# A planned RWKV and MLP kernel: four of its 24 units get their r and k turned by VectorE instead of TensorE, and the plan is searched in another way

## The chip, the cores and the metric

The kernel runs on one core of one Trainium2 chip. What counts is the device time of one execution in microseconds: the median over several runs. All engines of a core (TensorE or PE, VectorE or DVE, ScalarE or ACT, GpSimd or POOL, and SyncE or SP, which here only starts transfers) run at once, each through its own queue in order, and wait for one another by semaphores.

## What is computed

Two stages follow each other: a recurrent attention (RWKV5) over 768 steps, for 4 sequences with 8 heads of 48 numbers, and then a layer with 2048 hidden values on its 3072 rows of 384 numbers.

```python
def _attn_ref(r, k, v, w, u):
    B, H, S, D = r.shape                      # 4, 8, 768, 48
    state = np.zeros((B, H, D, D), dtype=np.float32)
    for t in range(S):
        kt, vt, rt = (k[:, :, t], v[:, :, t], r[:, :, t])
        cur = np.einsum('bhd,bhe->bhde', u[None] * kt, vt)
        y[:, :, t] = np.einsum('bhd,bhde->bhe', rt, state + cur)
        state = w[None, :, :, None] * state + np.einsum('bhd,bhe->bhde', kt, vt)
    return y

def _moe_ref(x, w_in, w_out):                 # 384 -> 2048 -> 384
    h = x @ w_in
    g = h - np.tanh(h)
    return (g @ w_out).astype(np.float32)
```

r, k and v are float32 on input; the two weight matrices come as float64 and are converted on the chip.

## The kernel before

**Units.** The attention is cut into 24 units. A unit is 64 steps of two sequences (z is 0 or 1), all heads: unit n has chunk n // 2 and the pair of sequences n % 2. Two units make a block of 256 rows for the layer, so there are 12 blocks j = 0 to 11, and block j needs units 2j and 2j + 1. Units of the same pair follow one another through their state.

A unit loads r, k and v with the steps on the partitions (`fetch`). It scales k by the powers of the decay (`kw`, DVE), and needs r and k once more with the head's 48 numbers on the partitions, r scaled by the powers of w, k by their inverse: `rT` and `kT`. Then TensorE makes r times state (`from_state`) and the products of r and k within the chunk (`levels`), DVE copies those below the diagonal into `at` under a mask (L981), the diagonal comes from `own`, `own_sum` and ScalarE's `diagonal`, and TensorE makes the outputs from `at` and v and the new part of the state from kw and v (`outputs`, `to_state`). ScalarE copies the result to `xt` and `rest`, and six small transfers on GpSimd's queue (`fill`, L931) put `rest` into xt; with that a block can be used.

**Two ways to turn.** In the first way, TensorE transposes r and kw into PSUM (`turn`, L795, two groups of four transposes per unit), DVE scales r from there (`scale_r`, L799, by the table `w_up`), and ScalarE copies k (`copy_k`, L832). In the other way, `spread_out` (L813) loads r and k a second time from DRAM in blocks of 32 steps by 32 numbers, eight transfers for r and eight for k on SP's queue, and DVE turns each 32 x 32 block and scales the whole (`across`, L818 and L819). The blocks lie in memory that the partial sums `parts` of the first six layer blocks used before. Here too r and k are loaded with the steps on the partitions, for kw and the diagonal. Between from_state and levels ScalarE reads one number of the PSUM bank (`between`, L872). Before the change, units 0 to 15 go the first way and 16 to 23 the other.

**The layer.** A tile is a block and two slices of 128 hidden values: TensorE makes h in PSUM (L169), ScalarE s, th, tg, q and small (squares, tanh and a mask), DVE g, c1, c2 and cp (L193 to L199), and TensorE multiplies g with w_out. There are 96 tiles. The first six blocks go through three passes, of 4, 4 and 8 slices; the partial sums of the first two lie in `parts`. In the first two passes the product with w_out is plain (o, L207). From the third pass on it is Strassen's scheme with seven products instead of eight (`products`, p, L258), for which GpSimd forms sums of g (`sums_of_g`, L243 to L247) and which collects its outputs on DVE (L286, L290 `gather`, the step that adds `parts` for the last time). It takes four PSUM banks, among them those of the first way's transposes, so the third pass begins only after the last unit of the first way has left them (`done`). The weights' conversion (L137 to L143) and the combinations of w_out (`mix`, L267) are work of DVE and ScalarE in the first 250 us.

**The order.** No loop sets the order. `near` adds every step to a `Plan` as a task with an engine, an assumed cost, its predecessors and a due time. `Plan.forward` lists the tasks by simulated time and due time, `backward` makes due times from a plan, and `search` moves due times at random and keeps what does not lengthen the planned span. `Plan.order` first searches 2500 times for the work that fits before 240 us (`BUSY`), then 500 times for the whole, then exchanges the tasks of units 16 to 23 for those of the other way (`change`), makes the due times after 240 us anew and searches 500 times there. Instructions are issued in the resulting order on each engine.

Of the kernel before, what the change touches and what calls it, by code (L numbers as in the profile page):

```python
# [31 lines left out]
C = 128  # L32
# [9 lines left out]
SEVEN = 8  # L42

# [258 lines left out]
class Plan:  # L302
# [12 lines left out]
    def __init__(self):  # L315
        self.tasks, self.fills, self.changes = [], [], []

    def add(self, engine, cost, run, after=(), due=1e9, data=0, gated=False, steps=0):
        t = SimpleNamespace(engine=engine, cost=cost, run=run, after=[x for x in after if x], due=due, data=data,
                            gated=gated, steps=steps, then=[], n=len(self.tasks))  # L320
        for x in t.after:
            x.then.append(t)
        self.tasks.append(t)
        return t

    def change(self, t, **new):

        self.changes.append((t, new))
# [149 lines left out]

    def order(self, first=2500, tries=500):
# [18 lines left out]
        self.search(due, tries, chance, 0.0)  # L498

        for t, new in self.changes:  # L500
            for x in t.after:
                x.then.remove(t)
            vars(t).update(new)
            t.after = [x for x in t.after if x]
            for x in t.after:
                x.then.append(t)
        for _ in range(4):
            plan = self.forward(self.due)
            latest = self.backward(plan)
            self.due = [old if start < self.BUSY else new for old, new, start in zip(self.due, latest, plan[1])]  # L510
        plan = self.search(self.due, tries, chance, self.BUSY)
# [28 lines left out]
def near(ctx, tc, r, k, v, w, u, out, shared, moe_w_in, moe_w_out):  # L540
# [20 lines left out]
    plan = Plan()  # L561
    add = plan.add
# [6 lines left out]

    spread = parts.rearrange("q a n -> q (a n)")  # L570
    blocks = [spread[:, i * 512 : (i + 1) * 512].rearrange("q (x b e) -> q x b e", x=2 * NP, b=SHORT // 32) for i in range(4)]
    again = spread[:, 2048 : 2048 + NP * (SHORT + 1)].rearrange("d (p n) -> d p n", p=NP)
# [83 lines left out]
    inverse = work.tile([128, NP, SHORT + 1], F32, name="inverse", tag="tg")  # L656
    w_up = fixed("w_up", [128, NP, 2, SHORT])
# [25 lines left out]
    def fills(to):  # L683
        def run(n):
# [6 lines left out]
    now = [add(e, 1.25 if e == "ACT" else .87, lambda e=e, at=at, x=x: e_of[e].dma_start(out=rows[at : at + NP, :, :D], in_=x.rearrange("(p i) d -> p i d", i=2)), due=-1, data=.05)  # L691
           for e, at, x in (("SP", 0, w), ("ACT", NP, u))]
    cols = add("PE", .25, lambda: T.transpose(cols_ps, rows.rearrange("p i d -> p (i d)"), ident[: 2 * NP, : 2 * NP]), now)


    now = add("DVE", .45, lambda: V.tensor_scalar(
        by[:, :, 1:], wcol[:, :, None].to_broadcast([128, NP, SHORT]), W_LOW, W_HIGH, ALU.max, ALU.min), [cols])
    now = add("DVE", .7, lambda: V.tensor_tensor_scan(
        power.rearrange(flat), by.rearrange(flat), plus.rearrange(flat), 0.0, ALU.mult, ALU.add), [now])

    ups = add("ACT", .6, lambda: A.copy(w_up, power[:, :, None, :SHORT].to_broadcast([128, NP, 2, SHORT])), [now])
    now = add("DVE", 1.75, lambda: V.reciprocal(inverse, power), [now])
    inverted = now
    doubled = add("ACT", .6, lambda: A.copy(twice, inverse[:, :, None, 1:].to_broadcast([128, NP, 2, SHORT])), [now])
    now = tabled = add("PE", .7, table, [doubled], steps=8)
    downs = add("ACT", .5, lambda: A.copy(w_down, tab.rearrange("s (h d) -> s h d", h=H)[:, :, :D]), [now])
    keeps = add("ACT", .2, lambda: A.copy(saved, cols_ps), [cols])
    w_us = add("POOL", .2, lambda: G.tensor_tensor(w_u, saved[:, :NP], saved[:, NP:], ALU.mult), [keeps])
    now = add("POOL", 1.0, bounds, [keeps])
    now = add("PE", .2, lambda: T.matmul(tab[0:1, 0:1], ok[:, 0, :1], shared["one"], start=True, stop=True), [now, downs])  # L710
    flagged = add("DVE", .15, lambda: V.tensor_scalar(shared["flag"], tab[0:1, 0:1], 128 * NP - 0.5, None, ALU.is_lt), [now])
    bonus = add("SP", .65, lambda: Q.dma_start(
        out=ub.rearrange("p h d -> p (h d)"),
        in_=bass.AP(tensor=u.tensor, offset=u.offset, ap=[[0, 128], [1, H * D]])), data=.7)

    add("ACT", 1.3, lambda: A.activation(fixed("warm", [128, 1]), shared["one"], AF.Tanh), due=0)


    def steps(generator):

        made = []

        def step():
            if not made:
                made.append(generator())
            next(made[0])

        return step

    loads, converted = [], []  # L730
    for n in range(weights.count):

        queues, data = (("SP",), (3.0,)) if n % 4 > 1 else (("SP", "POOL") * 2, (1.2, .95) * 2)
        of = [add(e, .55, lambda n=n, i=i, e=e: weights.load(n, i, e_of[e]), [converted[n - 4] if n >= 4 else None],
                  data=x, gated=True) for i, (e, x) in enumerate(zip(queues, data))]
        if weights.sources[n % 4 > 1].dtype != I64:
            converted.append(of[-1])
            continue
        step = steps(lambda n=n: weights.convert(n))
        now = of + ([converted[n - 2]] if n >= 2 else [])  # L740
        for name, cost in (("DVE", .47), ("DVE", .47), ("ACT", .84), ("ACT", .84), ("DVE", .87), ("DVE", .87), ("DVE", .87)):
            now = [add(name, cost, step, now)]
        converted += now


    def flat4(t):
        return t.rearrange("d p z t -> d (p z t)")

    def put(*args, **how):
        T.matmul(*args, skip_group_check=True, **how)  # L750

    units, filled, last_h = [], {}, {}

    def unit(n):
# [3 lines left out]
        ch, half = divmod(n, 2)  # L758
        j, slot = divmod(n, L)
        steps_at = slice(ch * SHORT, (ch + 1) * SHORT)  # L760
        t = SimpleNamespace(at=ats[n % 2])
        rt, vt, kw, state = rts[n % (AHEAD + 1)], vts[n % (AHEAD + 1)], kws[n % 2], states[half]
        two = n >= L * (FIRST + 2)
        pair = yk_ps if two else x_banks[n == 1]
        sign = -1.0 if slot and j in dense.negative else 1.0
        r_ps, k_ps = (pair[:, i] for i in range(2))
        lev, own_lev = (pair[:, :, at : at + 256].rearrange("s i (p t) -> s i p t", p=NP) for at in ((256, 0) if two else (0, 256)))
        none = SimpleNamespace(**{x: None for x in "r k v turn rT kw kT rk du own diag state lev cp out xt rest add decay".split()})
        b1, b2, b3 = (units[n - i] if n >= i else none for i in (1, 2, 3))
        x = SimpleNamespace(rest=None, rk=None, du=None, own=None)  # L770
        units.append(x)
        product = n < OWN
        swap = n >= SWAP


        direct = j == 0

        def fetch(name, src, after):
            def run(z):
                if name == "k" and not hasattr(t, "kt"):  # L780
                    t.kt = first_k[slot] if direct else load.tile([128, H, D], F32, name="kt", tag="kt")
                to = {"r": rt, "v": vt}.get(name)
                Q.dma_start(out=(t.kt if to is None else to)[HALF[z], :, :D],  # L783
                            in_=src[half * 2 + z, :, steps_at, :].rearrange("h t d -> t h d"))

            of = [add("SP", .65, lambda z=z: run(z), after, data=.71) for z in range(2)]
            return add("none", 0, lambda: None, of)

        x.r = fetch("r", r, [b3.turn, b3.rk, b1.r])
        x.k = fetch("k", k, [b3.kw, b3.rk, b1.k])  # L790
        x.v = fetch("v", v, [b3.out, b1.v])

        def turn(src, to):
            for p in range(NP):
                T.transpose(to[:, p * C : (p + 1) * C], src[:, 2 * p : 2 * p + 2, :].rearrange("t h d -> t (h d)"), ident)  # L795

        def scale_r():
            t.rT = work.tile([128, NP, 2, SHORT], F32, name="rT", tag="rT")
            V.tensor_tensor(flat4(t.rT), r_ps, flat4(w_up), ALU.mult)  # L799

        def scale_k():
            t.kT = work.tile([128, NP, 2, SHORT], F32, name="kT", tag="kT")
            V.tensor_tensor(t.kT, k_ps.rearrange("d (p z t) -> d p z t", p=NP, z=2),
                            inverse[:, :, None, 1:].to_broadcast([128, NP, 2, SHORT]), ALU.mult)
# [17 lines left out]
        def across_r():  # L822
            t.rT = across("rT", 0, power[:, :, :SHORT])
# [46 lines left out]
        def between():  # L870

            A.copy(seen, y_ps[:1, :, 0, 0])  # L872
# [552 lines left out]
```

## Time and profile before

| | us |
|---|---|
| median of three runs | 591.49 (590.93 to 591.64) |
| profiled execution | 591.61 |
| its span, first to last instruction | 589.5 |
| TensorE busy | 571.2 |
| weight loads busy (they overlap with matmuls) | 485.0 |
| VectorE busy | 484.1 |
| ScalarE busy | 398.9 |
| GpSimd busy | 208.3 |

The profile is of one execution. An engine's busy time is the union of its instructions' durations; ends of matmuls are modelled, so on TensorE the distance between starts says more than a duration. In lists of groups, a line has the source line, engine and operation, the tile written and those read, the shape, the count, the busy time, the mean in ns, and the engine's idle time just before. In the timeline a line has start, length, engine, line, operation, tiles and count, and in brackets how long the engine was idle before and which instruction released it. TensorE's small matmuls of a unit have the line of a helper, L750. The chain of waits is followed back from the last instruction.

### The profile page before, as it was taken

What the parts mean: (1) busy time and instruction counts of PE and PEld (TensorE: products, weight loads), DVE (VectorE), ACT (ScalarE), POOL (GpSimd) and SP (SyncE); (2) the same over time, 40 slices, a digit from 0 to 9 for tenths busy, and PEclk for the clock granted to TensorE, in tenths of its full rate; (3) what the DMA queues carried; (4) which work ended last, traced back from release to release, by engine and by line L of the source; (5) the groups of instructions that cost most, each with busy time, mean ns of one, the idle gap of its engine ahead of it and who ended that gap; (6) DMA issues with size and microseconds to landing.
All of it is one profiled execution on the core that took longest, in us unless ns stands there. A gap on an engine that the chain in (4) does not pass through costs nothing.

```text
span 589.5 us, 14312 instructions
## 1 busy us (share of the span) xinstructions
PE 571.2 (97%) x5525; PEld 485.0 (82%) x5525; DVE 484.1 (82%) x806; ACT 398.9 (68%) x894; POOL 208.3 (35%) x366
## 2 busy tenths in 40 slices
PE   8888999999999989999999999999999999999996
PEld 5566677777777768999999998989999888999995
DVE  5699969999999999988779889697775896555666
ACT  3698888989686975775555566565665785476652
POOL 6002212201000143555554544483344554363420
PEclk9999999999999999999999999999999999999999
DMA  6976995954411310203111412244121220100101
GB/s 118 201 155 129 161 204 107 126 132 86 93 54 28 62 30 21 39 16 61 36 26 24 85 28 30 40 83 69 35 30 19 38 40 1 25 11 2 28 1 31
DMA packets 121141, 36.91 MB, mean 63 GB/s; under 512 B 113352, under 2 KB 115496, under 8 KB 121064
## 3 DMA queue, kind: packets, MB, share of 16 engines
q1 hardware_dynamic: 115900, 28.73, 26.9%
q0 software_dynamic: 4992, 6.99, 5.4%
q8 instruction: 45, 0.74, 0.5%
q14 instruction: 32, 0.26, 0.1%
q10 hardware_dynamic: 172, 0.20, 0.1%
HBM read 30.08 MB, written 4.72 MB: 59 GB/s over the span
## 4 chain that ended last, share of the span: by engine, by line
PE 76%; DVE 11%; ACT 4%; issue 3%; DMA 3%; SPq 2%; POOL 0%; DVEq 0%; ACTq 0%; POOLq 0%
PE h L169 37%; PE p L258 27%; PE o L207 5%; PE yk_ps L750 5%; SPq L783 2%; DMA st<-in_moe_w_in_dram 2%; DVE tg L197 1%; DVE g L193 1%; DVE tg L195 1%; DVE g L199 1%; DVE rT L799 1%; ACT at L844 1%; ACT s L178 1%; PE x_ps L795 1%; DMA kt<-in_k_dram 1%
## 5 line engine op out<-in xcount | busy, mean ns | idle before, releaser
L169 PE MATMUL h<-xt,w_in_sb 128*128 128x256 f32 x1152 | 281.0, 381 | 1.1 <-DVE w_in_sb L143 0.9
L169 PEld LDWEIGHTS h<-xt,w_in_sb 128*128 128x128 f32 x1152 | 212.9, 190 | 31.4 <-PE x_ps L795 1.1
L243 POOL TENSOR_TENSOR sg<-g 128x256 f32<-128x256 f32 x69 | 53.8, 780 | 144.6 <-DVE g L199 72.5
L258 PE MATMUL p<-mixed,sg 128*128 128x192 f32 x426 | 104.0, 326 | 0.0
L193 DVE TENSOR_TENSOR g<-h,th 128x512 f32<-128x512 f32 x96 | 65.8, 685 | 33.2 <-ACT s L178 14.3
L182 ACT ACTIVATE tg<-h 128x512 f32<-128x512 f32 x96 | 57.2, 596 | 48.3 <-PE h L169 48.2
L195 DVE SCALAR_TENSOR_TENSOR tg<-s,tg 128x512 f32<-128x512 f32 x96 | 68.3, 712 | 25.9 <-ACT tg L182 13.8
L180 ACT ACTIVATE th<-h 128x512 f32<-128x512 f32 x96 | 57.4, 598 | 43.0 <-PE h L169 42.8
L931 POOL DMA_DIRECT2D xt<-rest x66 | 32.3, 496 | 146.0 <-ACT rest L910 146.0
L178 ACT ACTIVATE s<-h 128x512 f32<-128x512 f32 x96 | 57.4, 598 | 39.1 <-PE h L169 38.8
L199 DVE COPY_PREDICATED g<-small,tg 128x512 f32<-128x512 int32 x96 | 76.0, 793 | 4.0
L258 PEld LDWEIGHTS p<-mixed,sg 128*128 128x128 f32 x426 | 75.1, 190 | 0.0
L197 DVE SCALAR_TENSOR_TENSOR tg<-q,tg 128x512 f32<-128x512 f32 x96 | 68.5, 715 | 7.5 <-ACT q L184 4.1
L207 PE MATMUL o<-w_out_sb,g 128*128 128x384 f32 x192 | 69.8, 490 | 1.7 <-DVE g L199 1.6
L258 PE MATMUL p<-w_out_sb,g 128*128 128x192 f32 x284 | 71.1, 332 | 0.0
L184 ACT ACTIVATE q<-s,m1b 128x512 f32<-128x512 f32 x96 | 69.5, 724 | 0.8
L186 ACT ACTIVATE small<-s,smallb 128x512 f32<-128x512 f32 x96 | 69.3, 722 | 0.5
L258 PEld LDWEIGHTS p<-w_out_sb,g 128*128 128x128 f32 x284 | 52.5, 190 | 7.4
L844 ACT ACTIVATE at<-same,du 128x64 f32<-128x64 f32 x184 | 47.7, 343 | 5.7 <-DVE du L840 5.6
L207 PEld LDWEIGHTS o<-w_out_sb,g 128*128 128x128 f32 x192 | 35.5, 190 | 18.4 <-issue 1.9
L245 POOL TENSOR_TENSOR sg<-sg,g 128x128 f32<-128x128 f32 x69 | 44.6, 647 | 5.1
L247 POOL TENSOR_TENSOR sg<-sg,g 128x128 f32<-128x128 f32 x69 | 39.0, 566 | 5.1
(131 smaller groups left out, 684.4 us busy)
## 6 DMA issues: line engine op xcount, KB each, us to landing
st<-in_moe_w_out_dram SPq DMA_DIRECT2D x8, 768.0 KB, 5.4
rt<-in_r_dram SPq DMA_DIRECT2D x48, 96.0 KB, 3.3
vt<-in_v_dram SPq DMA_DIRECT2D x48, 96.0 KB, 2.9
st<-in_moe_w_in_dram SPq DMA_DIRECT2D x16, 288.0 KB, 5.1
kt<-in_k_dram SPq DMA_DIRECT2D x44, 96.0 KB, 3.3
out_dram<-o POOLq DMA_DIRECT2D x44, 96.0 KB, 2.3
st<-in_moe_w_in_dram POOLq DMA_DIRECT2D x16, 96.0 KB, 5.1
xt<-rest POOLq DMA_DIRECT2D x66, 16.0 KB, 2.3
```

What stands on the lines that cost most here:

```text
L169: self.nc.tensor.matmul(t.h2[:, z], self.w_in_sb[:, t.f // 2, kk, z * 128 : (z + 1) * 128], self.xts[t.j][:, kk].rearrange("p b t -> p (b ...
L178: A.activation(out, t.h, AF.Square)
L180: A.activation(out, t.h, AF.Tanh)
L182: A.activation(out, t.h, AF.Tanh, scale=G1)
L184: A.activation(out, t.s, AF.Square, bias=self.m1b)
L186: A.activation(out, t.s, AF.Relu, bias=self.smallb, scale=-1.0)
L193: V.tensor_tensor(t.g, t.h, t.th, ALU.subtract)
L195: V.scalar_tensor_tensor(t.tg, t.s, C4, t.tg, ALU.mult, ALU.mult)
L197: V.scalar_tensor_tensor(t.tg, t.q, K1, t.tg, ALU.add, ALU.mult)
L199: V.copy_predicated(t.g, t.small.bitcast(I32), t.tg)
L207: self.nc.tensor.matmul(self.outs[i], t.g2[:, z, i * C : (i + 1) * C], self.w_out_sb[:, t.f + z, :], start=t.first and z == 0, stop=t.last ...
L258: self.nc.tensor.matmul(ps[bank][:, half * n : (half + 1) * n], a, b, start=t.first and half == 0, stop=t.last, skip_group_check=True)
```

## The change

`lay_out` now builds a plan for a given number of early units and a way to turn the later ones. It is called twice: once with 16 early units and TensorE turning all (`simpler`), which is searched as before but never run, and once with 12 early units, all others loaded in blocks of 32 and turned by DVE. The second plan takes from the first the due times of all tasks that start before 90 us (`ALIKE`), makes the others from the tasks' own due times, and searches 500 times over what lies after 90 us.

Units 12 to 15 thereby leave the first way. The four buffers for blocks lie over `parts` of layer blocks 0 to 2 only, since the inverse powers now have a place of their own, and the first two turned units wait for the gathers of those three blocks; before, the first two waited for the last products of blocks 0 to 3 in the third pass. The third pass waits for unit 11 and not 15. `w_up` goes: r is scaled by the powers with a broadcast. A path that gives some of a unit's elementwise work to GpSimd (`eased`) is there but with `EASED = 12` and 12 early units no unit takes it. Assumed costs in the plan change for turning (1.22 to 1.4) and mixing (0.47 to 0.65).

```diff
+ALIKE = 90.0
+EASED = 12
...
-    def change(self, t, **new):
-
-        self.changes.append((t, new))
...
+    def follow(self, other, until, tries=500):
+
+
+        theirs = {t.key: (other.due[t.n], t.start) for t in other.tasks}
+        kept = [theirs[t.key][0] if theirs.get(t.key, (0, until))[1] < until else None for t in self.tasks]
+
+        def pinned(due):
+            return [y if y is not None else x for x, y in zip(due, kept)]
+
+        due = [t.due for t in self.tasks]
+        for t in reversed(self.tasks):
+            for x in t.then:
+                due[t.n] = min(due[t.n], due[x.n] - t.cost - self.HOP - (self.LANDS if t.data else 0))
+        for _ in range(5):
+            plan = self.forward(pinned(due))
+            due = self.backward(plan)
+        return self.listed(self.search(pinned(due), tries, Random(5), until))
+
...
-    inverse = work.tile([128, NP, SHORT + 1], F32, name="inverse", tag="tg")
-    w_up = fixed("w_up", [128, NP, 2, SHORT])
+    inverse = fixed("inverse", [128, NP, SHORT + 1])
...
+    def lay_out(early, across_by):
+
+        plan = Plan()
...
-    ups = add("ACT", .6, lambda: A.copy(w_up, power[:, :, None, :SHORT].to_broadcast([128, NP, 2, SHORT])), [now])
+        ups = add("ACT", .6, lambda: None, [now])
...
-        two = n >= L * (FIRST + 2)
+            two = n >= early
+            turned = two and across_by == "DVE"
...
-            V.tensor_tensor(flat4(t.rT), r_ps, flat4(w_up), ALU.mult)
+                V.tensor_tensor(t.rT, r_ps.rearrange("d (p z t) -> d p z t", p=NP, z=2),
+                                power[:, :, None, :SHORT].to_broadcast([128, NP, 2, SHORT]), ALU.mult)
...
-            if n == L * (FIRST + 2):
-                V.reciprocal(again, power)
-            t.kT = across("kT", 1, again[:, :, 1:])
+                t.kT = across("kT", 1, inverse[:, :, 1:])
...
-        x.turn = add("PE", .46, lambda: turn(rt, r_ps), [x.r] + free, steps=8)
-        if two:
-            freed = [tiles[y].o for y in parted[:4]] if n < L * (FIRST + 3) else []
-            plan.change(x.turn, engine="SP", cost=4.8, run=lambda: spread_out(r, 0), after=[b2.rT, *freed], data=.8, steps=0)
...
+            if turned:
+                freed = sum((gathered[y] for y in range(3)), []) if n < early + 2 else []
+                in_r = add("SP", 4.8, lambda: spread_out(r, 0), [b2.rT, *freed], data=.8)
+                in_k = add("SP", 4.8, lambda: spread_out(k, 1), [b2.kT, *freed], data=.8)
+            x.turn = None if turned else add("PE", .46, lambda: turn(rt, r_ps), [x.r] + free, steps=8)
...
-        x.rT = add("DVE", .62, scale_r, both + [ups])
-        if direct:
+            x.rT = add("DVE", 1.4, across_r, [in_r, b1.lev]) if turned else add("DVE", .62, scale_r, both + [ups])
+            if turned:
+                x.kT = add("DVE", 1.4, across_k, [in_k, b1.lev])
+            elif direct:
...
+                    gathered.setdefault(j, []).append(now)
...
-            done = units[L * (FIRST + 2) - 1]
+                done = units[early - 1]
...
-    for t in plan.order():
+    simpler = lay_out(L * (FIRST + 2), "PE")
+    simpler.order()
+    plan = lay_out(L * FIRST, "DVE")
+    for t in plan.follow(simpler, ALIKE):
```

## The prediction

> **What bounds the kernel now.** I read the page's busy shares first, then the chain that ended last, then the busy time in stretches of 20 us, and last the timeline of the stretch in which TensorE stops. From the page:
>
> ```profile
> PE 571.2 (97%) x5525; PEld 485.0 (82%) x5525; DVE 484.1 (82%) x806; ACT 398.9 (68%) x894; POOL 208.3 (35%) x366
> ...
> PE 76%; DVE 11%; ACT 4%; issue 3%; DMA 3%; SPq 2%; POOL 0%; DVEq 0%; ACTq 0%; POOLq 0%
> ```
>
> Three quarters of the chain are TensorE (PE), and PE is busy for 97%. A rule speaks against reading that as the bound: the Trainium skill (Trace Analysis, Identifying the Most-Contended Engine) calls PE's busy share a poor measure and wants the share of the weight loads, here 82%, the same as VectorE's (DVE). By that rule a fifth of PE could be free, and taking work from PE need not shorten anything. So I look at stretches and starts. The columns are PE, weight load, DVE, ACT and POOL busy, granted clock, DMA share and GB/s:
>
> ```profile
> 180.00:200.00 20.00, 20.00 (x260) 14.79 (x259) 19.31 (x32) 17.19 (x40) 0.00 (x0) 1.00 0.19 36
> 200.00:220.00 20.00, 18.24 (x204) 14.34 (x202) 20.00 (x32) 15.87 (x37) 8.89 (x14) 1.00 0.27 52
> 220.00:240.00 20.00, 19.81 (x217) 17.80 (x218) 19.38 (x35) 12.69 (x26) 7.42 (x13) 1.00 0.08 17
> ...
> 260.00:280.00 20.00, 20.00 (x108) 18.69 (x107) 15.32 (x26) 11.38 (x21) 10.72 (x17) 1.00 0.29 45
> ```
>
> The clock is full. From 120 us to 580 PE is at 20.00 of 20 nearly everywhere. Only from 200 to 240 it loses time, and there DVE is the full one. The timeline of PE says where:
>
> ```profile
> 200.60 0.60 PE L795 MATMUL x_ps<-ident,kw 128*128 128x128 f32 x4
> 201.03 1.46 PE L169 MATMUL h<-xt,w_in_sb 128*128 128x256 f32 x6
> 202.33 0.60 PE L795 MATMUL x_ps<-ident,rt 128*128 128x128 f32 x4
> 202.77 1.46 PE L169 MATMUL h<-xt,w_in_sb 128*128 128x256 f32 x6
> 204.06 1.45 PE L207 MATMUL o<-w_out_sb,g 128*128 128x384 f32 x4
> 205.35 1.46 PE L169 MATMUL h<-xt,w_in_sb 128*128 128x256 f32 x6
> 206.74 0.69 PE L750 MATMUL yk_ps<-rT,state 48*64 48x64 f32 x32
> 207.26 0.65 PE L750 MATMUL x_ps<-rT,kT 48*64 48x64 f32 x32
> 207.84 1.56 PE L169 MATMUL h<-xt,w_in_sb 128*128 128x256 f32 x6
> 210.75 0.66 PE L795 MATMUL x_ps<-ident,rt 128*128 128x128 f32 x4 [1.35 <-DVE at L981]
> ...
> 220.19 0.69 PE L750 MATMUL yk_ps<-rT,state 48*64 48x64 f32 x32 [0.59 <-DVE state L937]
> ```
>
> Starts tell more than durations: six matmuls of h run from 201.03 to 202.33, that is 1.30 us, and the next group begins at once. Six weight loads of 190 ns (their group's mean) fit under that, so the 82% are loads hidden behind the moving rows, not room. The two brackets are the only waits of a size after 120 us: 1.35 us for the masked copy at L981, 0.59 us for the state at L937, both on DVE, in the stretch where units 12 to 15 are squeezed in before the third pass. So PE's own work sets the end, plus 1.9 us lent to DVE.
>
> **The change, part by part.** Four units (12 to 15) go from the first way to the turned way, and from before the third pass to after its third block.
>
> *Transposes removed from PE.* Each of the four loses two groups of four (L795). A rule and a row differ on the price. The Trainium skill (TensorE: Matmul & The Clock Gate, Part 4: PE-mode transpose) gives about 275 ns for one in a kernel (measured for bf16), and the group's mean here, 278 ns, looks the same: 32 of them would be 32 x 0.275 = 8.8 us. The starts say otherwise: 200.60 to 201.03 is 0.43 us and 202.33 to 202.77 is 0.44 us for four, so 0.109 us for one; they overlap. I take the starts: 4 units x 2 x 0.435 = 3.5 us off PE, all on the bounding engine.
>
> *Waits removed.* 1.35 + 0.59 = 1.9 us. They go if DVE keeps up. In the seven stretches from 120 to 260 us DVE is busy 137.1 of 140. Out of that go, for each of four units, rT 0.684, kw 0.588, rk twice 0.576 and 0.597, du 0.543, the masked copy 0.726, state 0.547 and 0.561: 4.82 us, 19.3 in all. PE leaves the same stretch with four units less: transposes 0.87 and the four groups of small matmuls, by starts 0.52 + 0.58 for state and levels (206.74 to 207.84) and about 1.08 for the outputs, so 3.05 x 4 = 12.2 us, and the 1.9 of waits. That leaves 117.8 us of DVE in 125.9 us, 94% where it was 98%. So no wait of that kind is due: 1.9 us gained.
>
> *One more change of shape per unit.* Before, matmuls on the state and the levels of a unit follow each other; in the turned way a copy on ScalarE (L872) stands between, and PE does h or p meanwhile, so the small matmuls are entered three times and not twice. Entering costs 205.35 to 206.74 = 1.39 us for an h group that takes 1.29 to 1.30 elsewhere; leaving 1.40 (221.28 to 222.68). So 0.1 + 0.1 a visit. This is the rule that speaks against the change: the Trainium skill (TensorEngine Tiling (Array Packing), Key Properties) says that a change of tiling mode drains TensorE. It names no price; the row does: 4 x 0.2 = 0.8 us lost on PE. The 128x128 transposes show no such step (0.43 and 1.30).
>
> *DVE, ScalarE.* Each moved unit gains two turns and two scalings in place of one scaling of rT:
>
> ```profile
> L819 DVE TENSOR_TENSOR rT<-rT,power 128x512 f32<-128x512 f32 x8 | 6.0, 744 | 0.3
> ...
> L819 DVE TENSOR_TENSOR kT<-kT,parts 128x512 f32<-128x512 f32 x8 | 5.8, 730 | 0.3
> ...
> L818 DVE STREAM_TRANSPOSE rT<-parts 128x512 f32<-128x512 f32 x8 | 5.6, 699 | 0.0
> ...
> L818 DVE STREAM_TRANSPOSE kT<-parts 128x512 f32<-128x512 f32 x8 | 5.5, 692 | 0.0
> ```
>
> 0.744 + 0.730 + 0.699 + 0.692 - 0.684 = 2.18 us, times 4 is 8.7, less the second reciprocal (L827, 1.76): 7.0 us more on DVE. A whole turned unit is 4.14 + 2.87 = 7.0 us there. Units 12 and 13 (14.0 us) fall to 260 to 340 us, where DVE is idle for 4.7 + 5.4 + 2.7 + 3.6 = 16.3 us (four stretches); 14 and 15 fall to the next two blocks, where from 340 to 400 it has 7.5 us idle and 11.1 more to 440. Hidden, by 2 us in the tightest place; without that cover 2.18 us a unit would show. ScalarE loses four copies of kT (0.586) and gains four of 0.137: nothing on the path. Scaling rT by the broadcast power and not by w_up: kT by the broadcast inverse takes 686 ns against 684, nothing.
>
> *DMAs and queues.* Each moved unit adds 16 issues on SP, at 7.7 us for 16 (SP's timeline, 316.92 to 324.63), landing in 2.0 us. They wait for the gathers of blocks 0 to 2; behind them on SP stand later loads of v and k, due tens of us after. SP issues nothing from 281 to 317 and from 333 to 358: hidden. In the order that the changed program is built in, the gather of block 2 stands in tile 39 of 96, and unit 12's first turn on DVE in tile 42, at least two tiles or 9.7 us later; its eight issues and landing are 3.9 + 2.0 us. If they were late, the first turn would hold g, c1, c2 behind it in DVE's queue, and PE's p after them.
>
> *Block 6's deadline.* New: unit 13's last matmuls stand 1.5 tiles before block 6's first h. A tile is 4.87 us (chain: p at 231.57, 236.43, 241.30), plus unit 14's state and levels 1.1: 8.4 us. Within that ScalarE copies xt and rest (3 x 0.32 + 3 x 0.21 = 1.6 us), GpSimd issues six fills (2.9 us, timeline at 391.13) and they land in 2.3: 6.8 us. Margin 1.6 us; if ScalarE or GpSimd is in the midst of something, up to 1.6 is covered, the rest falls on PE. Nothing is taken for it.
>
> *The new search.* Up to 90 us the order is kept (it is the same up to tile 5). From there to 240 us DVE's conversions stand otherwise: up to tile 9, DVE's work summed with its groups' means is 35.5 us from tile 5 on, where it was 32.3; at tile 10 it is 38.9 against 38.7. The row that bounds it is 80 to 120 us, where DVE idles 2.7 + 0.4 us: so from 3 us lost to 1.2 us gained (two waits for the state at 88.7 and 96.8, 0.53 + 0.71, could vanish). I take zero, since the sums meet one tile later.
>
> **The sum.** -3.5 - 1.9 + 0.8 = -4.6 us. The profiled execution took 591.61 with a span of 589.5, 2.1 around it, which nothing here touches: span 584.9, execution 587.0. It lies 0.1 above the median of 591.49, so for the median I say 591.49 - 4.6 = **586.9**.
>
> **Rivals.** *The search gives half of it back* (chance 0.23): PE runs out of converted weights or of DVE between 90 and 130 us for 1 to 4 us. For it: 35.5 against 32.3 at tile 9. Against: levelled at tile 10. Time: 586.9 + 2.5 = 589.4, from 588.5 to 591. *Block 6 comes late* (0.12), the other side: unit 12 cannot begin before block 2 is gathered, and 12 and 13 must pass in sequence through DVE, PE, ScalarE and the fills before tile 48. Its price is what the chain is late beyond 1.6 us; it turns the gain into a loss once it is more than 1.6 + 4.6 = 6.2 us late, for instance if each of the turns holds DVE for 3 us; then some 593, up to 597. For it: only some seven tiles (34 us) of PE from the gather to block 6's first h and a chain per unit of DMA 10, DVE 3, and PE, ScalarE and copy about 7. Against: the second unit's DMAs run during the first. *Cheaper than thought* (0.10): the skill's price for transposes, or the waits before 120 us gone too, gives 591.5 - 7.5 = 584. *It does nothing* (0.05): DVE, not PE, sets the pace through the third pass, and PE's 3.5 us only become waits: 591.
>
> **Chances and range.** The likeliest case has 0.50, from 585.5 to 588.5. 0.2% of 591.5 is 1.2 us, about what a measurement of this kernel can tell from no change. Faster than 590.3: 0.50 + 0.10 + 0.19 of the half-lost case + 0.04 of the late one = 0.83. Within: 0.04 of the half-lost case + 0.05 = 0.09. Slower: 0.08. The range 584.0 to 591.0 leaves out the far end of the late block and of the cheap case.
>
> **What would show it.** L795 falls from 128 to 96 transposes; no wait of PE over 0.3 us between 120 and 260; three entries into the small matmuls for 12 units; DVE under 19 in each stretch from 140 to 240 and at 18 to 20 around 300 to 340; h of block 6 with no wait ahead of it. It would be wrong if PE waits for fills at block 6, if DVE stops at the first turn until SP's DMAs land, or if PE's busy time between 80 and 130 us drops.

## The result, and the profile after

| | before | after |
|---|---|---|
| median of five runs each, us | 591.64 (590.93 to 592.98) | 588.07 (587.41 to 588.50) |
| profiled execution, us | 591.61 | 587.71 |
| its span, us | 589.5 | 585.9 |
| TensorE busy, us | 571.2 | 570.1 |
| VectorE busy, us | 484.1 | 493.5 |

The changed kernel takes 0.9935 of the time before (95% interval 0.9919 to 0.9950). That is 3.6 us less by the medians of these runs; the forecast was 4.6 us less. The page of the changed kernel, busy shares and the chain that ended last:

```profile
PE 570.1 (97%) x5493; PEld 481.6 (82%) x5493; DVE 493.5 (84%) x817; ACT 395.6 (68%) x893; POOL 206.1 (35%) x366
...
PE 81%; DVE 9%; ACT 4%; issue 2%; DMA 2%; SPq 1%; POOL 0%; DVEq 0%; ACTq 0%; POOLq 0%
```

PE has 32 matmuls less (x5493 for x5525), DVE has 9.4 us more, and PE's part in the chain rises from 76% to 81%. Of the 3.6 us that the span is shorter, only some 1.0 are work of PE. The other 2.6 are idle time of PE (18.35 before, 15.75 after). Busy time in stretches of 20 us (PE, weight load, DVE, ACT, POOL, granted clock, DMA share, GB/s) shows part of it:

```profile
140.00:160.00 20.00, 20.00 (x78) 14.63 (x77) 19.84 (x31) 15.95 (x26) 0.00 (x0) 1.00 0.26 82
160.00:180.00 20.00, 20.00 (x80) 14.99 (x79) 19.93 (x33) 14.35 (x24) 0.00 (x0) 1.00 0.00 1
180.00:200.00 20.00, 20.00 (x78) 14.59 (x78) 19.04 (x33) 11.52 (x20) 2.70 (x4) 1.00 0.00 0
200.00:220.00 20.00, 19.35 (x100) 17.04 (x99) 19.41 (x32) 15.51 (x37) 8.30 (x12) 1.00 0.26 51
220.00:240.00 20.00, 20.00 (x108) 18.73 (x108) 19.34 (x33) 11.49 (x22) 10.45 (x16) 1.00 0.15 30
...
280.00:300.00 20.00, 20.00 (x249) 17.67 (x248) 18.24 (x32) 14.29 (x34) 10.58 (x16) 1.00 0.33 50
300.00:320.00 20.00, 20.00 (x250) 17.89 (x250) 19.25 (x34) 10.69 (x31) 10.95 (x19) 1.00 0.51 85
320.00:340.00 20.00, 20.00 (x277) 17.53 (x276) 17.83 (x32) 15.39 (x38) 7.37 (x13) 1.00 0.41 76
```

From 200 to 240 us PE now loses 0.65 us, where it lost 1.95. The moved units are where they were meant to be: from 280 to 340 PE has 249 to 277 matmuls per stretch instead of 109, most of them small ones, DVE is busy for 55.3 of 60 us instead of 48.3, and PE never stops. One gap remains in the first list, at the start of the third pass. PE's timeline there (start, length, engine, line, tiles, count, and in brackets idle time before and releaser):

```profile
201.80 1.46 PE L171 MATMUL h<-xt,w_in_sb 128*128 128x256 f32 x6
203.86 0.59 PE L260 MATMUL p<-w_out_sb,g 128*128 128x192 f32 x2 [0.60 <-DVE parts L222]
204.50 0.56 PE L260 MATMUL p<-mixed,sg 128*128 128x192 f32 x2
204.90 0.49 PE L260 MATMUL p<-mixed,g 128*128 128x192 f32 x2
205.22 0.49 PE L260 MATMUL p<-mixed,sg 128*128 128x192 f32 x2
205.55 1.46 PE L171 MATMUL h<-xt,w_in_sb 128*128 128x256 f32 x6
```

The third pass's first product waits for the last addition of the second pass's outputs to `parts` (L222, before L220). The wait is 0.60 us, and the eight products after it take 1.69 us (203.86 to 205.55) where eight a little later take 1.30 (209.11 to 210.41). DVE's timeline shows what stands ahead of the addition in DVE's queue; that it could have run earlier, a later experiment shows:

```profile
202.19 0.55 DVE L850 TENSOR_TENSOR rk<-rt,kt 128x384 f32<-128x384 f32 x1
202.66 0.68 DVE L195 TENSOR_TENSOR g<-h,th 128x512 f32<-128x512 f32 x1
203.26 0.54 DVE L222 TENSOR_TENSOR parts<-o,parts 128x384 f32<-128x384 f32 x1
```

The turns and scalings of the later units, now twelve of each, cost what they cost before (DVE's groups: busy us, mean ns, idle before):

```profile
L835 DVE TENSOR_TENSOR kT<-kT,inverse 128x512 f32<-128x512 f32 x12 | 8.7, 726 | 0.4
...
L835 DVE TENSOR_TENSOR rT<-rT,power 128x512 f32<-128x512 f32 x12 | 8.6, 714 | 0.4
L834 DVE STREAM_TRANSPOSE rT<-parts 128x512 f32<-128x512 f32 x12 | 8.4, 701 | 0.0
L834 DVE STREAM_TRANSPOSE kT<-parts 128x512 f32<-128x512 f32 x12 | 8.4, 700 | 0.0
```

The three entries into the small matmuls can be seen on the first moved unit, in PE's timeline of the changed kernel:

```profile
283.86 1.46 PE L171 MATMUL h<-xt,w_in_sb 128*128 128x256 f32 x6
285.25 0.69 PE L760 MATMUL yk_ps<-rT,state 48*64 48x64 f32 x32
285.87 1.56 PE L171 MATMUL h<-xt,w_in_sb 128*128 128x256 f32 x6
287.36 0.69 PE L760 MATMUL yk_ps<-rT,kT 48*64 48x64 f32 x32
287.99 0.59 PE L260 MATMUL p<-w_out_sb,g 128*128 128x192 f32 x2
288.42 0.49 PE L260 MATMUL p<-mixed,sg 128*128 128x192 f32 x2
```

By starts, from the first h to the first p it takes 4.13 us (283.86 to 287.99). Two groups of h account for 2.60 of it, and the first p is 0.1 longer (0.43 for 0.33): the state and the levels apart cost 1.63 us. Together, before the change, they took 0.52 + 0.58 us and an entry and a leaving of 0.1 each: 1.30 us. So a separation costs 0.33 us and not the 0.2 of the forecast. The two groups themselves are longer too, 0.62 and 0.63 us for 0.52 and 0.58.

Block 6, on which the other side's rival stood, has room. GpSimd's timeline has its six fills:

```profile
306.09 2.95 POOL L945 DMA_DIRECT2D xt<-rest  x6 [0.72 <-ACT rest L924]
```

PE's timeline has its first h:

```profile
315.35 1.46 PE L171 MATMUL h<-xt,w_in_sb 128*128 128x256 f32 x6
```

The last fill is issued at 309.0. These six land in 2.2 us (median), so it is there at about 311.2, 4 us ahead of h, and no bracket stands before h.

### The profile page after: what moved, and what is told of

Same layout as the page of the kernel before. It is cut to its first block, busy times and chain, and to the rows that moved or that the text cites. A ratio compares the mean times of both kernels' runs of the same rounds, so it can differ in the third digit from the quotient of the medians.

```text
span 585.9 us, 14391 instructions
## 1 busy us (share of the span) xinstructions
PE 570.1 (97%) x5493; PEld 481.6 (82%) x5493; DVE 493.5 (84%) x817; ACT 395.6 (68%) x893; POOL 206.1 (35%) x366
## 4 chain that ended last, share of the span: by engine, by line
PE 81%; DVE 9%; ACT 4%; issue 2%; DMA 2%; SPq 1%; POOL 0%; DVEq 0%; ACTq 0%; POOLq 0%
PE h L171 38%; PE p L260 27%; PE o L209 7%; PE yk_ps L760 6%; ACT at L858 1%; SPq L798 1%; DMA xt<-rest 1%; DVE g L201 1%; DVE tg L199 1%; PE h L688 1%; DVE g L195 1%; DVE power L144 1%; DVE at L993 1%; DMA first_k<-in_k_dram 1%; DVE tg L197 1%
## 5 line engine op out<-in xcount | busy, mean ns | idle before, releaser
L197 DVE SCALAR_TENSOR_TENSOR tg<-s,tg 128x512 f32<-128x512 f32 x96 | 70.2, 731 | 30.5 <-ACT tg L184 21.5
L201 DVE COPY_PREDICATED g<-small,tg 128x512 f32<-128x512 int32 x96 | 71.0, 740 | 4.0
L249 POOL TENSOR_TENSOR sg<-sg,g 128x128 f32<-128x128 f32 x69 | 41.4, 600 | 4.9
L247 POOL TENSOR_TENSOR sg<-sg,g 128x128 f32<-128x128 f32 x69 | 40.2, 582 | 4.9
```

The costliest lines, as they stand in the source:

```text
L197: V.scalar_tensor_tensor(t.tg, t.s, C4, t.tg, ALU.mult, ALU.mult)
L201: V.copy_predicated(t.g, t.small.bitcast(I32), t.tg)
```

## The experiments

In each comparison the kernel before ran on the same chip; its medians were 591.54, 591.45 and 591.80 us in the three sets. The changed kernel was not run again in them, so a difference from it is one between sets: taken by the ratios to before, which are ratios of means, it comes out up to 0.5 us otherwise than by the medians. My theory was the forecast's: PE's work sets the end, so the time falls by what leaves PE plus the two waits, less what the third entry costs. The rivals: the gain is due to the new search and not to the moved units; the transposes cost another price; what ended the waits was another order on DVE and not less work.

**Is it the units or the search? Sixteen early units, new search.** `across_by` stays DVE for units 16 to 23, and everything else is as in the changed kernel.

```diff
-EASED = 12
+EASED = 99
...
-    plan = lay_out(L * FIRST, "DVE")
+    plan = lay_out(L * (FIRST + 2), "DVE")
```

> The second plan is laid out with 16 early units instead of 12, so all four moved units are back in the first way, while the new search (order kept to 90 us, the rest searched anew) stays; the path that gives elementwise work to GpSimd is kept off. Theory (the moved units make the gain): the time of before, 591.6 within 1.2 us. Rival (the new search made the gain): about 588.1, as the changed kernel. Halfway, 589.8, would give each a half.

Measured: 590.19 us, 0.9980 (0.9971 to 0.9989), between the two expected times. Without the moved units the new search gains 1.4 us; the moved units then bring the other 2.1 to 2.7, by medians and by ratios. But this was one draw of a random search, which a later run shows.

**Half of it: fourteen early units** (`FIRST + 1` in the same line).

> 14 early units, so two of the four go back to the first way. Theory: half of the gain is lost, between 589.3 and 590.3. If the gain comes from the third pass starting free of unit 15's chain on DVE, fourteen loses little: 588.1 to 588.8, since half of that load is gone too. If the search decides: anywhere between 587 and 592.

Measured: 590.18 us, 0.9977 (0.9968 to 0.9986), the same as with sixteen. If each moved unit were worth the same, it should have come out half-way. This run can't settle it: as later runs show, another start of the search alone moves the time by more than that.

**The price of a transpose on PE.** In the kernel before, the transposes of units 12 to 15 are each done three times; the repetition writes the same values again. That adds 64.

```diff
+        def again_and_again(src, to):
+            for _ in range(3 if n >= L * FIRST else 1):
+                turn(src, to)
...
-        x.turn = add("PE", .46, lambda: turn(rt, r_ps), [x.r] + free, steps=8)
+        x.turn = add("PE", .46, lambda: again_and_again(rt, r_ps), [x.r] + free, steps=8)
```

(and the same for `turn_k`)

> The kernel before, with each transpose of units 12 to 15 done three times into the same place: 64 more transposes, the order kept. By the starts (0.109 us each) PE has 7.0 us more; up to 1.9 of it can lie in the two waits on DVE: 5.1 to 7.0 us slower than before, 596.7 to 598.6. By the price of 0.275 us each: 17.6 less 1.9, so 15.7 to 17.6 us slower, about 608.

Measured: 596.72 us, 1.0093 (1.0078 to 1.0109), which is 5.2 us more. PE's timeline of this kernel:

```profile
203.49 1.47 PE L795 MATMUL x_ps<-ident,kw 128*128 128x128 f32 x12
204.80 1.46 PE L169 MATMUL h<-xt,w_in_sb 128*128 128x256 f32 x6
...
214.27 1.53 PE L795 MATMUL x_ps<-ident,rt 128*128 128x128 f32 x12 [0.23 <-DVE at L985]
```

Twelve take 1.31 us from start to start, 0.109 each: 7.0 us for 64. The wait for the masked copy, which was 1.35 before, is 0.23 here, and the idle time of PE from 180 to 260 us falls from 1.99 to 0.23. So 1.8 us of the added work filled waits, and 7.0 - 1.8 = 5.2 is what was measured. The price by starts is right, and 275 ns (17.6 us for 64) is out. It also shows that in this stretch work on PE and waits for DVE stand in for each other: the two terms -3.5 and -1.9 of the forecast are not independent where they lie side by side.

**What a further entry into the small matmuls costs.** In the changed kernel, outputs and the new part of the state of ten turned units are parted by PE's next task, as state and levels are.

```diff
-                if not direct:
+                if not direct and not turned:
...
+            if turned and more:
+                now.apart = to_state
...
+        listed.append(t)
+        if t.engine == "PE":
+            listed += held
+            held = [SimpleNamespace(engine="PE", start=t.start, run=t.apart)] if hasattr(t, "apart") else []
```

> The changed kernel, where the ten turned units that still add to the state make this part (16 small matmuls) after PE's next task instead of right after the outputs: ten more visits to the small matmuls, no work added, the rest of the order kept. If a visit costs what the timeline of the changed kernel shows for the levels set apart (0.1 to enter, 0.1 to leave and 0.1 to 0.15 of overlap lost, 0.35 us): 3.5 us slower, 591.6. By the prediction's 0.2: 2.0 us slower, 590.1. If visits are hidden: 588.1.

Measured: 592.78 us, 1.0022 (1.0013 to 1.0032), which is 4.7 us over the changed kernel, more than any of the expectations: 0.47 us for each of ten. Two waits of 0.4 us appear that the changed kernel does not have (for the state and for the squares s); without them it is 0.39. PE's timeline of this kernel:

```profile
293.34 0.69 PE L760 MATMUL yk_ps<-at,vt 64*64 64x64 f32 x32
293.97 0.59 PE L260 MATMUL p<-w_out_sb,g 128*128 128x192 f32 x2
294.40 0.49 PE L260 MATMUL p<-mixed,sg 128*128 128x192 f32 x2
294.72 0.49 PE L260 MATMUL p<-w_out_sb,sg 128*128 128x192 f32 x2
295.14 0.68 PE L760 MATMUL yk_ps<-vt,kw 64*64 64x48 f32 x32
295.75 1.56 PE L171 MATMUL h<-xt,w_in_sb 128*128 128x256 f32 x6
```

The six products between take 1.17 us (293.97 to 295.14), where 0.33 for each two makes 0.98: 0.1 at each end, as forecast. On top of that the small groups are 0.63 and 0.61 long. So a visit costs the changes of shape and some 0.1 more that is lost where two small groups no longer overlap, and the sum is 0.33 to 0.47 us.

**The new wait at the third pass.** In the changed kernel the last addition at L222 goes two places ahead in DVE's queue.

```diff
+    listed = list(plan.follow(simpler, ALIKE))
+    at = next(i for i, t in enumerate(listed) if getattr(t, "mark", None) == (FIRST - 1, SEVEN, 1))
+    moving = listed.pop(at)
+    to = [i for i, t in enumerate(listed[:at]) if t.engine == "DVE"][-2]
+    listed.insert(to, moving)
```

> The changed kernel with one instruction moved: the last addition to parts before the third pass goes two places ahead in DVE's queue. If the wait of PE for it (0.60 us in the bracket, and the slow first two groups of p after it, 1.0 us in all) is on the path: 587.1, faster by 0.6 to 1.0. If another wait stands behind it: 588.1.

Measured: 587.51 us, 0.9933 (0.9920 to 0.9945). PE's timeline of this kernel, at the same place:

```profile
201.67 1.46 PE L171 MATMUL h<-xt,w_in_sb 128*128 128x256 f32 x6
202.96 0.49 PE L260 MATMUL p<-w_out_sb,g 128*128 128x192 f32 x2
203.29 0.56 PE L260 MATMUL p<-mixed,sg 128*128 128x192 f32 x2
```

The wait is gone, and so is the slow first pair. The median is 0.6 us lower than the changed kernel's, by the ratios only 0.1; the intervals overlap, so the trace shows that the wait went, and that time was gained is not shown. From 220 to 260 us PE now loses 0.18 us where it lost 0.04. Moving in addition one masked copy of tile 9 (`cp`, wait of 0.53 us at 116.10) ahead of a conversion:

```diff
+    at = next(i for i, t in enumerate(listed) if getattr(t, "m", None) == 8)
+    moving = listed.pop(at)
+    to = [i for i, t in enumerate(listed[:at]) if t.engine == "DVE"][-1]
+    listed.insert(to, moving)
```

> The changed kernel with two instructions moved in DVE's queue: the addition to parts as in the earlier run, and tile 9's last step ahead of one conversion (0.9 us), for which PE waits 0.53 us at 116. If DVE's order and not its load costs PE these waits: 587.5 less 0.4 to 0.9, so 586.6 to 587.1. If DVE's load sets that stretch: 587.5 as with one move.

Measured: 587.42 us, 0.9931 (0.9916 to 0.9945), the lowest median of all, and no different from the one before it. The wait for a masked copy now stands ahead of 118.81 us and is 0.82 us long, so this move only shifted it.

**How near block 6 is to being late.** In the changed kernel the four buffers lie one step further along `parts`, so that the first moved units wait for the gathers of blocks 0 to 3 and not 0 to 2.

```diff
-    blocks = [spread[:, i * 512 : (i + 1) * 512]...
+    blocks = [spread[:, 1024 + i * 512 : 1024 + (i + 1) * 512]...
...
-                freed = sum((gathered[y] for y in range(3)), []) if n < early + 2 else []
+                freed = sum((gathered[y] for y in range(4)), []) if n < early + 2 else []
```

> The changed kernel, but the four buffers for blocks lie one step further along parts, so that the first two turned units wait for the gathers up to block 3 instead of block 2, about 19.5 us later. If block 6's deadline has the slack the trace shows (unit 13's fills land about 4 us ahead, and unit 12's loads begin at 246), PE waits at block 6 for some 10 to 15 us: 598 to 603. If the deadline doesn't bind at all: 588 to 589.

Measured: 595.38 us, 1.0066 (1.0050 to 1.0081), which is 7.3 us over the changed kernel, between the two expectations. PE's timeline of this kernel:

```profile
299.59 0.69 PE L760 MATMUL yk_ps<-rT,state 48*64 48x64 f32 x32 [1.23 <-DVE rT L835]
...
320.09 0.69 PE L760 MATMUL yk_ps<-rT,state 48*64 48x64 f32 x32 [1.61 <-DVE state L951]
...
321.06 0.69 PE L760 MATMUL yk_ps<-rT,kT 48*64 48x64 f32 x32 [0.27 <-ACT seen L886]
...
322.67 1.04 PE L760 MATMUL yk_ps<-at,vt 64*64 64x64 f32 x32 [0.91 <-DVE at L993]
323.46 1.06 PE L760 MATMUL yk_ps<-vt,kw 64*64 64x48 f32 x32
324.46 1.01 PE L260 MATMUL p<-w_out_sb,g 128*128 128x192 f32 x2
325.26 0.85 PE L260 MATMUL p<-mixed,sg 128*128 128x192 f32 x2
325.90 0.66 PE L260 MATMUL p<-mixed,g 128*128 128x192 f32 x2
326.40 0.49 PE L260 MATMUL p<-mixed,sg 128*128 128x192 f32 x2
```

Its busy time in stretches, two of 20 us and three of 1 us (columns as above):

```profile
300.00:320.00 20.00, 18.48 (x316) 15.95 (x308) 19.40 (x35) 14.16 (x43) 7.73 (x13) 1.00 0.46 69
320.00:340.00 20.00, 18.72 (x314) 16.04 (x315) 15.64 (x30) 11.82 (x35) 9.28 (x18) 0.91 0.50 85
...
323.00:324.00 1.00, 1.00 (x50) 1.00 (x44) 0.89 (x2) 0.00 (x0) 0.92 (x2) 0.50 0.43 50
324.00:325.00 1.00, 1.00 (x22) 0.91 (x19) 0.40 (x1) 0.39 (x2) 0.24 (x1) 0.50 0.42 61
325.00:326.00 1.00, 1.00 (x5) 1.00 (x4) 0.16 (x1) 0.97 (x4) 0.00 (x0) 0.50 0.05 4
```

One block later, and units 12 and 13 come too late: first PE waits for the scaled rT, then for each step of the units' own chain, 4.0 us in all. After the last wait PE is slow: by starts, the two small groups and three pairs of products take 3.73 us (322.67 to 326.40), where they take 0.63 + 0.61 + 0.43 + 0.33 + 0.33 = 2.33 in the outputs' splitting above; the granted clock of the stretch is 0.91, because it is 0.50 from about 323 to 326 us. That is 1.4 us more. Another 0.9 us of idle time lie between 60 and 120 us (PE busy 57.69 for 58.55). The last 1.0 of the 7.3 us is not placed; the profiled execution has the clock at 0.50 once more, from 26 to 29 us, where the changed kernel's has 1.00, and part of it may lie there. The rival "Block 6 comes late" was thus a real mechanism with the right sign, one block away; it did not decide.

**How much is the search's luck?** The same kernel with another start of the random search, twice, and with more tries:

```diff
-        return self.listed(self.search(pinned(due), tries, Random(5), until))
+        return self.listed(self.search(pinned(due), tries, Random(6), until))
```

(and `Random(7)`; and `tries=2000` for 500 with `Random(5)`)

> The changed kernel with another start of the random search, nothing else. If the search's luck is worth less than the gain: within 1 us of 588.1. If luck is of the gain's size: up to 4 us away.

> As the run before, with a third start of the random search. Within 1 us of 588.1 if luck is small; up to 4 us away if it is as large as the gain. Together with the other two it gives the spread of the search.

> The changed kernel with 2000 instead of 500 tries in the second plan's search. If the search is short of a better order: 586 to 587.5. If what is left (visits, waits by DVE's order) is not in what the plan counts: 587.5 to 588.7.

And sixteen early units with `Random(6)`:

> 16 early units with the new search, as in the earlier run (590.2), from another start of the search. If the new search by itself is worth 1.4 us against before: 589.8 to 590.7. If that was luck: nearer to 591.5 or further away.

| units in the first way | search | us | ratio to before (95%) |
|---|---|---|---|
| 12 | as changed | 588.07 | 0.9935 (0.9919 to 0.9950) |
| 12 | Random(6) | 588.08 | 0.9937 (0.9924 to 0.9950) |
| 12 | Random(7) | 588.86 | 0.9956 (0.9943 to 0.9969) |
| 12 | 2000 tries | 589.78 | 0.9969 (0.9956 to 0.9982) |
| 16 | as changed | 590.19 | 0.9980 (0.9971 to 0.9989) |
| 16 | Random(6) | 591.85 | 1.0004 (0.9996 to 1.0013) |

By their medians all twelve-unit orders are faster than both sixteen-unit ones, but the nearest two (2000 tries, and sixteen as changed) lie 0.1% apart and their intervals overlap. The means of the ratios are 0.9949 and 0.9992: the moved units are worth 0.43%, 2.5 us. Four and two orders are few, and within each kind they lie 1.7 us apart. A second start gave nothing of the first experiment's 1.4 us, so that gain is as likely a lucky draw as a gift of the new search, and the changed kernel has one of the two better orders of four. The longer search was slower than either expectation. It keeps only what does not lengthen the planned span, so its plan is no longer than the changed kernel's, and still the real time is 1.7 us more: its trace has waits of 1.03 and 1.10 us on PE, ahead of 298.4 and 354.0 us (for a state and for a masked copy).

The profiles of these orders also tell work and waits of PE apart:

| units in the first way | search | PE busy, us | PE idle 120 to 260 us | PE idle 260 to 560 us |
|---|---|---|---|---|
| 16 | kernel before | 571.15 | 1.99 | 0.01 |
| 16 | as changed | 571.51 | 1.67 | 0.00 |
| 16 | Random(6) | 572.25 | 1.04 | 0.00 |
| 14 | as changed | 570.63 | 1.30 | 0.80 |
| 12 | as changed | 570.15 | 0.69 | 0.00 |
| 12 | Random(6) | 570.36 | 0.19 | 0.63 |
| 12 | Random(7) | 569.62 | 1.10 | 0.00 |
| 12 | 2000 tries | 570.30 | 0.24 | 2.24 |

PE's work is 1.5 us less with twelve units (means 570.1 and 571.6), and no twelve-unit order has more than any sixteen-unit one. From 120 to 260 us it waits 1.0 us less (0.56 and 1.57), but in two of the four orders the moved units bring waits of their own after 260 us, so that from 120 to 560 us only 0.3 us remain (1.27 and 1.57). With fourteen, PE's work is 570.6, in between as the theory has it, and 2.10 us of waits, more than in any order with sixteen, stand against it. So it is PE's smaller work that holds over the orders; what becomes of the waits depends on the order.

**Is it DVE's order or its load that made PE wait?** In the kernel before, unit 14's masked copy (wait of 1.35 us) goes two places ahead in DVE's queue.

```diff
+    listed = list(plan.order())
+    moving = units[14].cp
+    at = listed.index(moving)
+    listed.pop(at)
+    to = [i for i, t in enumerate(listed[:at]) if t.engine == "DVE"][-2]
+    listed.insert(to, moving)
```

> The kernel before, with one instruction moved: unit 14's masked copy (L981), for which PE waits 1.35 us at 210.75, goes two places ahead in DVE's queue, past a mix and a c2 (about 1.5 us). If this wait is worth its length on the path: 1.0 to 1.35 us faster than before, 590.2 to 590.5. If DVE's other work is what PE needs next, so that the wait only moves: within 0.4 us of before.

Measured: 593.18 us, 1.0020 (1.0009 to 1.0032): no gain, but 1.4 us more, which neither expectation had. The profiled execution took 591.23. PE's timeline of it:

```profile
219.74 0.69 PE L750 MATMUL yk_ps<-rT,state 48*64 48x64 f32 x32 [2.03 <-DVE state L937]
```

The wait at 210 us is gone, and the one for the state has grown from 0.59 to 2.03: together 1.94 before and 2.03 now. This move only shifted the wait, and the profiled execution is 0.4 us shorter than that of the kernel before. The median is not: three executions with a mean granted clock of 0.998 or more took 590.93 to 591.31, the nine others, at 0.993 to 0.997, took 592.62 to 594.37. In the same set only three of the 24 executions of the kernel before are below 0.998. So the 1.4 us go with a lower clock; none of the nine was profiled, and whether the longer wait brings it about is not shown.

That DVE's load alone sets this stretch does not follow from one move: sixteen units in the order of `Random(6)` wait 1.04 us from 120 to 260 where the kernel before waits 1.99, with DVE still busy for 134.9 of the 140 us. Order and load both count; another order took up to 0.95 us of these waits away, and the moved units on average 1.0.

Not tried: joining the state's and the levels' matmuls again by leaving out the read by ScalarE between them. Whether the result would still be right without it, no run shows.

## Why the prediction was right, and where it was not

The sign and the bound were right: PE sets the end, and 3.6 us came where 4.6 were forecast. The place was right in part: of the profiled 3.6 us, 1.0 are work of PE and 1.3 waits from 180 to 260 us. By its steps:

- *Transposes removed from PE* (-3.5): right. L810 (before L795) has 96 transposes for 128, and 64 extra ones cost 0.109 each. The group's mean (280 ns) is a length in the pipeline and not a price, and the page's 275 ns for one (Trainium skill, TensorE: Matmul & The Clock Gate, Part 4: PE-mode transpose) is no price for four in a row either. The price in the rival "Cheaper than thought" falls with it.
- *Waits removed* (-1.9): the two named waits went, but the term was too large and its reason weak. What failed is "So no wait of that kind is due". In the 125.9 us from 120 us on, for which 117.8 us of DVE were forecast, DVE is busy for 122.2, so 97% and not 94%, and "DVE under 19 in each stretch from 140 to 240" was wrong in all five. The sum took 19.3 us of single durations from a busy time. DVE's durations overlap in the record, as the lines of 202.19 to 203.73 show (0.47 us from a start to the next for a length of 0.55): before the change, those from 120 to 260 add up to 155 us within 137.1 busy. By that share, an estimate, 19.3 us of durations are 17.0 of busy time, which is about half of the 4.4 us; the rest is other work of DVE that stands there now, and is not settled. A wait was left at the addition at L222, 0.60 us, where the third pass begins. From 180 to 260 us PE's idle time fell by 1.30 (1.99 to 0.69), not by 1.9, and the slow first products cost 0.4 more. Over all orders the waits are 1.0 us less from 120 to 260 and 0.3 less from 120 to 560 us.
- *One more change of shape per unit* (+0.8): the mechanism was right, the size was off. The 0.2 counted the two changes; it left out the overlap of two small groups that follow each other. It measures 0.33 by starts and 0.39 to 0.47 by ten added partings, so 1.3 to 1.9 us for four units. That a change of tiling drains TensorE (Trainium skill, TensorEngine Tiling (Array Packing), Key Properties) agrees with the 0.1 at each end; the 0.1 beyond it came out of the runs.
- *DVE, ScalarE; DMAs and queues* (0): right. DVE has 9.4 us more, 7.0 of them forecast, and PE is busy for 160.00 of the 160 us from 260 to 420. That is this order's luck too: with `Random(6)` and with 2000 tries PE waits 0.63 and 2.24 us from 260 to 560, for DVE in each wait that the profile names. SP issued the loads of unit 12 and r of unit 13 from 245.82 to 259.2 us, and only k of unit 13 after a pause, at 265.69, when block 2's gather was done. At the first turn (275.88) unit 12's had landed long before.
- *Block 6's deadline* (0): right, with a margin of 4 us instead of 1.6. Copies, fills and landing take 7.0 us, as forecast (6.8); but from the end of unit 13's matmuls (304.19) to block 6's first h PE has 11.2 us of work and not 8.4. One block later cost 7.3 us.
- *The new search* (0): near the mean of two sixteen-unit orders (0.9992, 0.5 us), but its range was as real as its mean. Orders of the same kind lie 1.7 us apart, and that the built one is among the better is luck.

In the profiled pair, PE's busy time fell by 1.0: -3.5 for transposes, +1.3 to +1.9 for partings, +0.4 for slow first products, which makes -1.8 to -1.2. Its idle time fell by 2.6: 1.3 from 180 to 260, 0.6 from 60 to 120 (waits of 0.53, 0.71 and 0.18 are gone, 0.32 and 0.53 are new), and 0.9 in the first 60 us, less 0.3 late. The 0.9 are not the change's: in executions of the kernel before and two with its order up to there, PE is busy for 50.4, 50.9 and 51.3 of the first 60 us. So the steps give some 2.5 to 3 us for this order. The means over the orders give 2.5 us by the times, of which PE's work (1.5) and its waits from 120 to 560 us (0.3) make 1.8. The rest up to 3.6 lies within what the search and single executions vary, and is not settled further.

"The search gives half of it back" did not come: 60 to 120 us gained 0.6. "It does nothing" is out for the mean of the orders; for the slowest twelve-unit one it is not far off, since 2.24 us of waits appear there after 260 us.

## What to carry to other kernels

When the bounding engine runs without gaps, price what leaves it by the distance of starts, and what is split on it by the starts of the whole sequence, with the lost overlap and not only the switches. Durations that overlap must not be taken from a busy time one by one. Where a second engine is above 95% in a stretch, count a removed wait only in part: of three moved instructions here one took a wait away and two only shifted it, and another order brings other waits. Before crediting an effect of half a per cent to an edit in a kernel whose order comes from a random search, run other starts of the search with and without the edit.

## What the runs showed of the hardware that was not expected

TensorE's granted clock can fall to a half for some 3.4 us after a wait of about 2 us, and the same wait does not always do it. In the kernel with the blocks one step later, PE stood still for 1.61, 0.27 and 0.91 us within 4.2 us, and what followed took 3.73 us instead of 2.33 (0.79 us by starts for a group of small matmuls that takes 0.63 elsewhere, then 1.00 for 0.61 and 0.80 for 0.43), with the granted clock at 0.50 from about 323 to 326 us. A single wait can be followed by the same: in the kernel with both instructions moved, the clock is at 0.50 from 26 to 28 us after this one:

```profile
24.30 0.66 PE L810 MATMUL x_ps<-ident,kw 128*128 128x128 f32 x4 [2.10 <-DVE kw L966]
```

It is so in three profiles (waits of 2.06, 2.10 and 2.25 us at this place); in three others, with waits of 2.34, 2.25 and 2.18 us there, the clock stays at 1.00, as it does in the profiled execution with the wait of 2.03 us at 219.74. What decides was not tested. A half clock for 3.4 us of 590 makes 0.003 of an execution's mean clock, so an estimate from these traces reads 0.997 as one such fall and 0.994 as two: the profiles with one and with two have just these means.

Two groups of 32 small matmuls take some 0.15 us less when the one follows the other (0.52 + 0.58) than apart (0.62 + 0.63), beyond the changes of shape at their ends.
